# Twenty small unread products ahead of the second unit's mask

## The chip, the cores and the metric

The kernel runs on one core of a Trainium2 chip. The metric is the device time of one execution in microseconds (us): the kernel before takes 485.94 us, the median of three runs (485.89 to 486.22).

## The reference

Three layers follow one another. A windowed attention (4 batches, 8 heads, 576 positions, 64 wide; half of the heads look at the last 32 positions, half at every fourth of the last 128) gives 2304 tokens of 512. A gated layer makes `sigmoid(x @ w_gate) * (x @ w_val)` of 1536 and multiplies that with `w_out`. A soft mixture of 8 experts with 4 slots each follows:

```
scores = scale * (q @ k.T), masked;  x = softmax(scores) @ v
h = sigmoid(x @ w_gate) * (x @ w_val);  y = h @ w_out
logits = y @ phi;  d = softmax over tokens;  c = softmax over slots
out = c @ experts(d.T @ y)      # relu(. @ w1[e]) @ w2[e]
```

## The kernel before, in words

The tokens are worked through in five blocks (four of 512 tokens, a last one of 256). The attention of a block is four *units* of two heads. A unit is loaded as `qk` and `v` (L259 to L280). `scores` (L140) takes two banks of `ps_a` (four banks in all), lays the mask into each with a product against an identity in bfloat16 (L148), and adds 32 small float32 products, 32 x 64 each (L162). In the trace each of these is two passes, and each pass is a weight load and a product, so that the scores of a unit are 128 instructions for TensorE. `softmax` (L172) runs on VectorE and ScalarE, `turn_unit` (L191) transposes the weights through a bank (L195), and `weighted` (L198) makes 32 small products with `v` (L222), again 128 instructions. `finish_unit` (L227) splits the result into a high and a low part (L250, L251).

The gated layer is `l1` (L462): for a column tile `f` and for gate and value, twelve products of 128 x 512 (L474). Its weights arrive packed, are converted (`convert`, L371, on ScalarE, VectorE and GpSimd), stored, and loaded again (L365, L369, L866); all transfers are issued by SyncE in one queue. Between the two halves of a column tile `l1` calls a function that issues one step of the attention of the next blocks, so that from about 36 to 205 us TensorE alternates between a dozen large products and the two bursts of 128 small ones (scores of one unit, `weighted` of an earlier one). In the same stretch `slot_weights` (L404) adds transposes (L412), and small products (L418, L427). Blocks 2 and 3 are done as a pair with sums of halves (L606, L596), then the last block, and the experts with their weights (`load_e`, L816) end the program.

At the start there is nothing to interleave. `keep_warm` (L108) and L113 issue products of zeros until the first loads land. Then the four units of block 0 come one after the other, TensorE waiting for each unit's `qk`. A scheduler orders the instructions of each engine here; each engine then executes its own list in that order.

In what follows a *step* is one instruction of TensorE, a weight load or a product. The list of all steps lies in memory and is fetched by a DMA queue of its own (`q8 instruction` in the profile).

Of the kernel before, what the change touches and what calls it, by code (L numbers as in the profile page):

```python
# [31 lines left out]
C0 = 21  # L32
C1 = 19
WP = 1
ND = 4
M_ID, M_COLS = 768, 896
C_ID, C_I4, C_PHI, C_COLS = 0, 128, 256, 384
# [8 lines left out]
def k_window(n, hp, t, i):  # L46
    if n < 4:
        return 32 * (4 * t + i) if hp < 2 else 160 * i + 32 * t
    return 160 * t + 32 * i if hp < 2 else 64 * (4 * t + i)
# [7 lines left out]
def tile_kernel(  # L57
# [10 lines left out]
    nc = tc.nc  # L68
# [14 lines left out]
    def b8(tag, shape, dt, name):  # L83
        return big.tile(shape, dt, tag=tag, name=name, bufs=BUFS[tag])
# [6 lines left out]
    i4 = ones32[:, 0:32]  # L91
    phi = cst[:, C_PHI - C_ID : C_COLS - C_ID].rearrange("p (k s) -> p k s", k=ND)
    acc = cpool.tile([P, 3, 512], F32, name="acc")
# [14 lines left out]
    def keep_warm(count):  # L108
        for _ in range(count):
            nc.tensor.matmul(idle, lhsT=zero[:, 0:P], rhs=zero[:, 512:1024], start=True, stop=True)  # L110

    keep_warm(WARM)
    for i in range(SMALL):  # L113
        g = slice(32 * (i % 4), 32 * (i % 4) + 32)
# [18 lines left out]
    units = {}  # L133
# [3 lines left out]
    def at(ins):  # L137
        return tc.keep_in_program_order(ins) if grouped[0] else ins

    def scores(u, ts):  # L140
        n, hp = u["id"]
        q, k = u["qk"][:, 0:512], u["qk"][:, 512:1536]
        if "s_ps" not in u:
            u["bank"] = [ps_a.tile([P, 512], F32, tag="a", name=f"s_ps{r}") for r in range(2)]
            u["s_ps"] = [x[:, 0:256].rearrange("p (t c) -> p t c", t=4) for x in u["bank"]]
            for r in range(2):
                at(
                    nc.tensor.matmul(  # L148
                        u["s_ps"][r].rearrange("p t c -> p (t c)"),
                        lhsT=msk[:, M_ID:M_COLS],  # L150
                        rhs=mask[:, 2 if n == 4 else (1 if hp >= 2 else 0)],
                        start=True,
                        stop=False,
                        skip_group_check=True,
                    )
                )
        for t in ts:
            for i in range(4):
                for r in range(2):
                    o = k_window(n, hp, t, i)  # L160
                    at(
                        nc.tensor.matmul(  # L162
                            u["s_ps"][r][32 * i : 32 * i + 32, t, :],
                            lhsT=q[64 * r : 64 * r + 64, 128 * t + 32 * i : 128 * t + 32 * i + 32],
                            rhs=k[64 * r : 64 * r + 64, o : o + 64],
                            start=False,
                            stop=True,
                            skip_group_check=True,
                        )
                    )  # L170
# [56 lines left out]
    def finish_unit(u):  # L227
# [3 lines left out]
        def part(x, y):  # L231
            return x[:, hp].rearrange("p (t y x) -> p t y x", t=2, y=2)[:, :, y]

        if n in (2, 3):
            if n not in xf:
                xf[n] = b8("xa", [P, ND, 512], F32, "xf")
            nc.scalar.copy(part(xf[n], 0), xp[0])
            nc.vector.tensor_copy(part(xf[n], 1), xp[1])
            return
        if n not in x_hi:  # L240
            if n == 4:
                x4 = b8("x4", [P, 2, ND, 256], F32R, "x4")
                x_hi[n], x_lo[n] = x4[:, 0], x4[:, 1]
            else:
                tag = "xb" if n % 2 else "xa"
                x_hi[n] = b8(tag, [P, ND, 512], F32R, "x_hi")
                x_lo[n] = b8(tag, [P, ND, 512], F32R, "x_lo")
        for y in range(2):
# [10 lines left out]
    def attn_steps(pbs, norm, head=None):  # L259
# [34 lines left out]
        def s_step(z, ts=range(4)):  # L294
            if z == 0 and 0 in ts:
                if head:
                    load_qk(0)
                    ld(nc.sync.dma_start(msk, masks.bitcast(BF16)))
                    load_qk(1)
                    ld(nc.sync.dma_start(cst, consts))  # L300
                    load_v(0)
                    load_qk(2)
                    load_v(1)
                    head()
                    load_qk(3)
                    load_v(2)
                    load_v(3)
                else:
                    first(load_qk)
                    first(load_v)  # L310
            scores(us[z], ts)
            if 3 not in ts:
                return
            if 2 <= z and not head:
                weighted(us[z - 2], range(2), us[z])
            softmax(us[z], norm)
            load(z + 2, load_qk)
            if z == 0:
                load(2, load_v)
# [4 lines left out]
        def p_step(z, ts=range(2)):  # L324
            if head or z + 2 >= len(us):
                weighted(us[z], ts)
            if head:
                keep_warm(WP)
            if 1 in ts:
# [74 lines left out]
    def slot_weights(f, wo_f, lag):  # L404

        wt = pm.rearrange("p a b -> p (a b)").rearrange("p (k c x) -> p k c x", k=ND, c=2)
        at_ = {}
# [573 lines left out]
    for f in range(NF):  # L981
        for j in range(2):
            ins = T.matmul(
                lt_ps[32 * j : 32 * j + 32],
                lhsT=wp[:, f],
                rhs=g_sb[4, f][:, P * j : P * j + P],
                start=(f == 0),
                stop=(f == NF - 1),
# [96 lines left out]
    for f in range(NF):  # L1085
# [3 lines left out]
                lhsT=acc[:, f // 4, P * (f % 4) : P * (f % 4) + P],  # L1089
                rhs=i4w,  # L1090
                start=True,
                stop=True,
# [29 lines left out]
    for e in range(8):  # L1122
        for h in range(2):
            for kc in range(ND):
                ins = T.matmul(  # L1125
                    h_ps[h][32 * kc : 32 * kc + 32],
                    lhsT=st[:, kc, 32 * e : 32 * e + 32],
                    rhs=ew[0, e, h][:, kc],
                    start=(e == 0),
                    stop=(e == 7),  # L1130
# [227 lines left out]
```

## Time and profile before

| | |
|---|---|
| median of three runs | 485.94 us |
| profiled execution, its own time | 487.55 us |
| its span, first to last instruction | 485.8 us |
| TensorE products busy (PE) | 465.4 us, 96% |
| TensorE weight loads (PEld) | 358.1 us, 74% |
| VectorE, ScalarE, GpSimd | 64%, 44%, 32% |
| mean granted TensorE clock | 0.987 |

Busy products overlap, so 96% does not mean that TensorE runs at its peak. The granted clock is 1.00 or 0.50 of full speed in a stretch. "<-issue" behind an idle time means that the engine waited for nothing that the profile shows as an instruction or a transfer of data.

### The profile page before, as it was taken

What the parts mean: (1) busy time and instruction counts of PE and PEld (TensorE: products, weight loads), DVE (VectorE), ACT (ScalarE), POOL (GpSimd) and SP (SyncE); (2) the same over time, 40 slices, a digit from 0 to 9 for tenths busy, and PEclk for the clock granted to TensorE, in tenths of its full rate; (3) what the DMA queues carried; (4) which work ended last, traced back from release to release, by engine and by line L of the source; (5) the groups of instructions that cost most, each with busy time, mean ns of one, the idle gap of its engine ahead of it and who ended that gap; (6) DMA issues with size and microseconds to landing.
All of it is one profiled execution on the core that took longest, in us unless ns stands there. A gap on an engine that the chain in (4) does not pass through costs nothing.

```text
span 485.8 us, 12812 instructions
## 1 busy us (share of the span) xinstructions
PE 465.4 (96%) x5480; PEld 358.1 (74%) x5480; DVE 310.2 (64%) x629; ACT 213.6 (44%) x413; POOL 155.5 (32%) x132
## 2 busy tenths in 40 slices
PE   6789999999999999999999999999999999999993
PEld 3567888778777878787778888888888889842552
DVE  3869888758688666466876656656547765532623
ACT  2455555444455553454355554554535334300222
POOL 0244455325554564612033333324211124210100
PEclk9889999999999999999999999999999999999997
DMA  8978969994989792222220220201499886689976
GB/s 314 418 279 315 354 240 325 323 326 154 373 301 357 243 337 99 88 88 71 105 77 12 86 66 22 88 12 74 144 376 424 356 316 236 236 320 352 427 260 241
DMA packets 23721, 112.14 MB, mean 231 GB/s; under 512 B 2288, under 2 KB 7152, under 8 KB 14576
## 3 DMA queue, kind: packets, MB, share of 16 engines
q1 hardware_dynamic: 23664, 111.32, 62.0%
q8 instruction: 43, 0.70, 0.6%
q14 instruction: 14, 0.11, 0.1%
HBM read 97.16 MB, written 14.16 MB: 229 GB/s over the span
## 4 chain that ended last, share of the span: by engine, by line
PE 73%; DVE 4%; issue 2%; ACT 2%; POOL 2%; DMA 1%; DVEq 0%; ACTq 0%; POOLq 0%
PE l1ps L474 21%; PE pa L596 13%; PE pe L596 6%; PE tp L729 4%; PE so_ps L1187 3%; PE pd L596 3%; PE h_ps L1125 3%; PE sp L754 2%; PE lt_ps L700 2%; PE s_ps L222 2%; PE s_ps L162 2%; POOL fw L386 1%; PE wt_ps L412 1%; PE tr L195 1%; PE op L1225 1%
## 5 line engine op out<-in xcount | busy, mean ns | idle before, releaser
L474 PE MATMUL l1ps<-x_hi,whl 128*128 128x512 f32 x384 | 130.0, 403 | 2.4 <-ACT x_hi L250 2.0
L474 PEld LDWEIGHTS l1ps<-x_hi,whl 128*128 128x128 f32 x384 | 72.2, 189 | 18.5 <-ACT x_hi L250 2.7
L474 PE MATMUL l1ps<-x_lo,whl 128*128 128x512 f32 x192 | 76.0, 396 | 0.0
L386 POOL TENSOR_TENSOR fw<-fw 128x512 int32<-128x512 int32 x36 | 49.0, 1368 | 63.5 <-DVE fw L385 27.5
L474 PEld LDWEIGHTS l1ps<-x_lo,whl 128*128 128x128 f32 x192 | 36.4, 190 | 6.7 <-DVE x_lo L251 0.2
L460 DVE SCALAR_TENSOR_TENSOR g<-g,l1ps 128x512 f32<-128x512 f32 (+1 forms) x36 | 21.4, 593 | 25.3 <-PE l1ps L474 25.1
L474 PE MATMUL l1ps<-x,whl 128*128 128x256 f32 x288 | 37.0, 285 | 0.0
L474 PEld LDWEIGHTS l1ps<-x,whl 128*128 128x128 f32 x288 | 35.4, 192 | 0.4 <-ACT whl L437 0.2
L484 ACT ACTIVATE g<-l1ps 128x512 f32<-128x512 f32 (+1 forms) x36 | 18.9, 526 | 33.9 <-PE l1ps L474 33.7
L438 POOL TENSOR_TENSOR whl<-w,whl 128x512 fp32r<-128x512 f32 x12 | 15.9, 1329 | 51.2 <-ACT whl L437 39.7
L383 ACT ACTIVATE fw<-st 128x512 f32<-128x512 f32 x36 | 22.9, 676 | 12.2 <-DMA st<-wd 12.2
L729 PEld LDWEIGHTS tp<-cst,g 128*128 128x128 f32 x192 | 21.3, 140 | 5.4 <-issue 4.1
L729 PE MATMUL tp<-cst,g 128*128 128x128 f32 x192 | 25.0, 275 | 0.0
L384 DVE TENSOR_SCALAR fw<-fw 128x512 uint32<-128x512 uint32 x36 | 23.4, 659 | 2.4 <-ACT fw L383 1.7
L438 POOL TENSOR_TENSOR whl<-wst,whl 128x512 fp32r<-128x512 f32 x12 | 16.3, 1359 | 26.7 <-ACT whl L437 21.7
L734 ACT COPY gt<-tp 128x512 f32<-128x512 f32 x24 | 14.1, 586 | 24.1 <-PE tp L729 21.4
L659 DVE TENSOR_TENSOR tm<-pe,tm 128x512 f32<-128x512 f32 x12 | 8.3, 692 | 24.6 <-PE pe L596 24.6
L385 DVE TENSOR_SCALAR fw<-st 128x512 int32<-128x512 uint32 x36 | 18.1, 534 | 7.5 <-DMA st<-wd 7.2
L438 DVE TENSOR_TENSOR whl<-fw,whl 128x512 fp32r<-128x512 f32 x24 | 20.6, 873 | 3.5 <-ACT whl L437 2.9
L176 DVE TENSOR_REDUCE mx<-s_ps 128x4 f32<-128x256 f32 x40 | 15.3, 414 | 10.1 <-PE s_ps L162 8.2
L437 ACT CAST whl<-fw 128x512 fp32r<-128x512 f32 x24 | 14.6, 620 | 15.0 <-POOL fw L386 10.5
L189 POOL TENSOR_TENSOR sm<-sm,su 128x512 f32<-128x512 f32 x12 | 14.6, 1218 | 18.6 <-DVE su L188 16.3
(481 smaller groups left out, 961.7 us busy)
## 6 DMA issues: line engine op xcount, KB each, us to landing
ew<-w SPq DMA_DIRECT2D x32, 1024.0 KB, 7.5
st<-wd SPq DMA_DIRECT2D x18, 1024.0 KB, 9.3
wst<-wg SPq DMA_DIRECT2D x12, 1024.0 KB, 6.5
v<-qkv SPq DMA_DIRECT2D x20, 512.0 KB, 6.0
wg<-fw SPq DMA_DIRECT2D x12, 512.0 KB, 7.7
w<-wg SPq DMA_DIRECT2D x6, 1024.0 KB, 6.7
qk<-qkv SPq DMA_DIRECT2D x10, 576.0 KB, 5.8
qk<-qkv SPq DMA_DIRECT2D x8, 528.0 KB, 5.0
```

Source lines behind the costliest of these rows:

```text
L176: nc.vector.tensor_reduce(mx[:, 4 * r : 4 * r + 4], u["s_ps"][r], AX.X, ALU.max)
L189: norm.tensor_tensor(s, s, su.unsqueeze(2).to_broadcast([P, 8, 64]), ALU.mult)
L383: nc.scalar.activation(top, st[:, c, 1].bitcast(F32), AF.Prelu, scale=2.0**-112, alpha=2.0**32)
L384: nc.vector.tensor_scalar(top.bitcast(U32), top.bitcast(U32), 3, None, ALU.logical_shift_left)
L385: nc.vector.tensor_scalar(low.bitcast(I32), st[:, c, 0], 2.0**-29, None, ALU.mult)
L386: nc.gpsimd.tensor_tensor(low.bitcast(I32), top.bitcast(I32), low.bitcast(I32), ALU.add)
L438: (nc.gpsimd if pool[h] else nc.vector).tensor_tensor(whl[:, 1, h], src[:, h], whl[:, 0, h].bitcast(F32), ALU.subtract)
L460: return nc.vector.scalar_tensor_tensor(g, g, 1.0, val, ALU.add, ALU.mult)
L474: nc.tensor.matmul(pt[:, 0:nt], lhsT=whl[:, w_, a, dc, :], rhs=x_[n][:, dc, :], start=first, stop=(dc == HP_ORDER[-1] and w_ == 1),)
L484: nc.scalar.activation(g, pt[:, 0:nt], AF.Tanh, scale=0.5)
L596: nc.tensor.matmul(pt, lhsT=w[:, w_, P * c : P * c + P], rhs=x_[:, c], start=first and c == 0 and w_ == 0 and x_ is hi, stop=c == 1 and w_ ...
L729: nc.tensor.transpose(tp[:, c], g_sb[self.n, 4 * q + c][:, P * j : P * j + P], ident)
```

## The change

Ahead of the mask of the second unit (block 0, position 1 of its order) twenty products of 32 x 8 are issued into columns 256 to 263 of the unit's two banks, which nothing reads. They multiply slices of the first unit's `qk`, which is in place by then. Each is float32, so two passes of a weight load and a product: 80 steps in all. The dictionary `units` only keeps the first unit at hand.

```diff
+PAD = 20
...
+    def pad_stream(banks, qk):
+        for i in range(PAD):
+            r, g = i % 2, i // 2 % 4
+            at(
+                nc.tensor.matmul(
+                    banks[r][32 * g : 32 * g + 32, 256:264],
+                    lhsT=qk[64 * r : 64 * r + 64, 32 * g : 32 * g + 32],
+                    rhs=qk[64 * r : 64 * r + 64, 512:520],
+                    start=True,
+                    stop=True,
+                    skip_group_check=True,
+                )
+            )
...
             u["s_ps"] = [x[:, 0:256].rearrange("p (t c) -> p t c", t=4) for x in u["bank"]]
+            units[n, u["z"]] = u
+            if (n, u["z"]) == (0, 1):
+                pad_stream(u["bank"], units[0, 0]["qk"])
```

On TensorE, at the end of the first unit's scores (banks `s_ps_191` and `s_ps_192`), the list before goes on with the mask of the second unit (banks 238 and 239):

```order
L162 MATMUL s_ps_191<-qk 32x64
L162 MATMUL s_ps_192<-qk 32x64
L148 LDWEIGHTS msk
L148 MATMUL s_ps_238<-msk 128x256
L148 LDWEIGHTS msk
L148 MATMUL s_ps_239<-msk 128x256
L162 MATMUL s_ps_238<-qk 32x64
```

The list of the changed kernel has the twenty products there (the lines of `scores` are numbered 18 higher):

```order
L180 MATMUL s_ps_191<-qk 32x64
L180 MATMUL s_ps_192<-qk 32x64
L145 MATMUL s_ps_238<-qk 32x8
L145 MATMUL s_ps_239<-qk 32x8
...
L166 LDWEIGHTS msk
L166 MATMUL s_ps_238<-msk 128x256
L166 LDWEIGHTS msk
L166 MATMUL s_ps_239<-msk 128x256
L180 MATMUL s_ps_238<-qk 32x64
```

Everything behind keeps its order on TensorE and stands 80 steps later in the list.

On VectorE, in the softmax of the first three units (`mx` is the maximum of a bank of scores, `su` a unit's sum), the list before has both sums, of units 0 and 1, ahead of the third unit's first maximum (bank 333):

```order
L178 TENSOR_TENSOR sm_172<-s_ps_239,mx 128x256 [waits DVE_49]
L186 TENSOR_REDUCE su<-sm_172 128x8 [waits Activation_49] x2
L187 TENSOR_SCALAR su<-su 128x8 [waits DVE_49]
L176 TENSOR_REDUCE mx<-s_ps_333 128x4 [waits PE_49]
L188 RECIPROCAL su<-su 128x8 [waits DVE_49]
```

In the changed kernel's list (the third unit's bank is 353 there) that maximum stands between the two sums:

```order
L196 TENSOR_TENSOR sm_172<-s_ps_239,mx 128x256 [waits DVE_49]
L204 TENSOR_REDUCE su<-sm_172 128x8 [waits Activation_49]
L194 TENSOR_REDUCE mx<-s_ps_353 128x4 [waits PE_49]
L205 TENSOR_SCALAR su<-su 128x8 [waits DVE_49]
L204 TENSOR_REDUCE su<-sm_172 128x8 [waits Activation_49]
L206 RECIPROCAL su<-su 128x8 [waits DVE_49]
```

The second unit's sum has moved behind a wait for the third unit's scores. ScalarE, GpSimd and SyncE keep their lists.

## Rows read from the trace of the kernel before

**Rows 1.** The page: busy time of TensorE, the instruction queue (packets, MB, share).

```profile
PE 465.4 (96%) x5480; PEld 358.1 (74%) x5480; DVE 310.2 (64%) x629; ACT 213.6 (44%) x413; POOL 155.5 (32%) x132
q8 instruction: 43, 0.70, 0.6%
```

**Rows 2.** Timeline of TensorE's products: start, us, operation, count [idle before].

```profile
11.82 0.90 PE L162 MATMUL s_ps<-qk 64*32 64x64 f32 x55 [0.65 <-issue]
23.93 0.42 PE L222 MATMUL xp<-pt_ring,v 64*64 64x32 f32 x13 [1.14 <-issue]
127.38 0.36 PE L222 MATMUL s_ps<-pt_ring,v 64*64 64x32 f32 x9 [0.68 <-issue]
155.84 0.30 PE L222 MATMUL s_ps<-pt_ring,v 64*64 64x32 f32 x2 [0.77 <-issue]
```

**Rows 3.** Stretches cut there: us; PE, PEld, DVE, ACT, POOL (count); PEclk; DMA; GB/s.

```profile
0.00:11.50 11.50, 7.63 (x223) 3.77 (x224) 4.65 (x12) 2.54 (x3) 0.20 (x4) 1.00 0.86 306
11.50:23.30 11.80, 9.46 (x255) 6.26 (x254) 9.58 (x27) 5.24 (x10) 2.67 (x2) 0.86 1.02 421
23.30:127.10 103.80, 100.56 (x1529) 80.38 (x1529) 80.20 (x162) 52.22 (x99) 46.31 (x35) 0.98 0.83 296
127.10:155.50 28.40, 27.69 (x509) 22.41 (x509) 24.46 (x48) 16.35 (x31) 14.30 (x12) 1.00 0.92 336
```

**Rows 4.** DMA view, 9.4 to 10.4 us: instruction queue's packets, MB, share.

```profile
q8 instruction: 1, 0.02, 6.1%
```

**Rows 5.** DMA view, 153.4 to 154.4 us.

```profile
q8 instruction: 1, 0.02, 5.9%
```

**Rows 6.** DMA view, 140 to 146.8 us (it has no row of the instruction queue).

```profile
DMA packets 402, 2.36 MB, mean 348 GB/s; under 512 B 39, under 2 KB 39, under 8 KB 188
```

**Rows 7.** DMA view, 146.9 to 148 us.

```profile
q8 instruction: 1, 0.02, 5.5%
```

**Rows 8.** Stretches around the two times of lower granted clock.

```profile
8.90:12.30 3.40, 1.37 (x62) 0.82 (x63) 2.61 (x7) 0.78 (x2) 0.00 (x0) 1.00 1.03 420
12.40:15.70 3.30, 3.30 (x28) 1.44 (x14) 2.98 (x10) 0.67 (x1) 0.00 (x0) 0.50 1.01 415
22.60:25.90 3.30, 1.85 (x30) 1.26 (x23) 2.40 (x7) 2.14 (x5) 0.00 (x0) 1.00 1.03 410
26.00:29.40 3.40, 3.40 (x59) 2.55 (x61) 3.34 (x7) 1.39 (x3) 2.15 (x2) 0.50 0.91 308
```

**Rows 9.** Timeline of TensorE's products in block 0's units.

```profile
6.75 0.39 PE L148 MATMUL s_ps<-msk 128*128 128x256 bf16 x2
7.86 0.86 PE L162 MATMUL s_ps<-qk 64*32 64x64 f32 x64 [0.71 <-DMA qk<-qkv]
8.65 0.61 PE L110 MATMUL idle<-pm 128*128 128x512 bf16 x2
10.85 0.32 PE L162 MATMUL s_ps<-qk 64*32 64x64 f32 x9 [1.38 <-DMA qk<-qkv]
15.61 0.67 PE L195 MATMUL tr<-cst,sm 128*128 128x128 f32 x4
```

**Rows 10.** Timeline of VectorE in the softmax of those units.

```profile
8.74 0.76 DVE L176 TENSOR_REDUCE mx<-s_ps 128x4 f32<-128x256 f32 x2 [0.35 <-PE s_ps L162]
13.53 0.69 DVE L189 TENSOR_TENSOR sm<-sm,su 128x512 f32<-128x512 f32 x1
```

**Rows 11.** Stretches of the middle: a pair of bursts, what follows it, and a later one.

```profile
143.10:145.55 2.45, 2.45 (x138) 1.88 (x136) 2.34 (x4) 0.51 (x1) 1.36 (x1) 1.00 0.99 403
145.55:152.82 7.27, 7.27 (x44) 6.05 (x40) 6.42 (x14) 5.66 (x11) 2.48 (x2) 1.00 1.00 415
172.50:174.00 1.50, 1.50 (x32) 1.42 (x26) 1.50 (x4) 0.07 (x1) 1.50 (x2) 1.00 0.75 212
```

**Rows 12.** Timeline of TensorE's products around 171 us.

```profile
170.88 0.86 PE L162 MATMUL s_ps<-qk 64*32 64x64 f32 x64
172.73 0.63 PE L427 MATMUL wp_ps<-cst,acc 128*128 128x32 f32 x4
```

## The prediction

> **What bounds the kernel now.** I read the page first, then the waits of TensorE, then its timeline and stretches cut where it stood still. TensorE's products are busy for 465.4 of 485.8 us [rows 1], and in the middle, where two bursts of 128 small steps alternate with large products, without a gap [rows 11]. So what TensorE loses there is lost at the end. In four places it stands in the middle of a burst and waits for nothing that the profile knows: "<-issue" of 0.65, 1.14, 0.68 and 0.77 us [rows 2].
>
> The reader is to see what these places have in common, by counting. Stretches cut inside the pauses hold 447, 509, 3058 and 1018 steps (PE plus PEld) [rows 3]. With 3, 14 and 6 further entries of the list, which the view doesn't count (I take them for the separate waits in front of products that wait for two engines), the last three are 512, 3072 and 1024: 2, 12 and 4 times 256. The instruction queue moves 0.70 MB in 43 packets, 16.3 KB each, against 10,960 steps, 255 per packet [rows 1]. So TensorE's list comes in blocks of 256 entries, and each pause is the wait for the next block. I number the boundaries from the first pause: 0, 2, 14 and 18 paused the engine.
>
> When is a block late? One is fetched between 9.4 and 10.4 us [rows 4], 6.1% of 16 engines over 1 us, so 0.98 us long, and TensorE goes on at 11.82, 1.4 us after it; one between 153.4 and 154.4 [rows 5], and TensorE goes on at 155.84 [rows 2], 1.4 us after it again. So a block can be executed 2.4 us after its fetch begins. The fetch begins when TensorE has passed the boundary before, or later: boundary 17 lies at the mask at 152.8 (counting 256 entries back from 155.84), and the fetch at 153.4 followed by 0.6 us; boundary 16 lies 256 entries further back, past the 84 steps of 145.55 to 152.82 and 172 of the 274 before them, so some 100 steps into that pair of bursts, 143.6 [rows 11], and the fetch that followed came at 146.9 [rows 6, 7], 3.3 us later, at a DMA share of 0.99. A block that is executed in less than 3.0 to 5.7 us pauses the engine; a pair of bursts, 256 steps, takes 2 us.
>
> [...]
>
> **The change part by part.** The twenty products: 64 passes of L162 take 0.86 us [rows 9], so 40 take 0.54. They stand behind the first unit's scores, ahead of the mask at 6.75 [rows 9], and the 0.71 us wait for the second unit's load covers them: 0, and 0.54 if the cover were gone. They wait for nothing new. All that follows keeps its order, but each boundary now falls 80 entries earlier in the work. I go through all 42 and compare, in the timeline, when TensorE gets there with the earliest time of the block.
>
> *Removed.* Boundaries 14 and 18 move 80 steps up, still in the same burst, and the boundary before moves too, so that the block between them begins among the large products: block 18 then runs from L412 at 145.6 [rows 11] into the burst that ends at 156, over 8 us, and block 14 likewise. The pauses of 0.68 and 0.77 go: -1.45. Nothing else is late there, TensorE being gapless.
>
> *Block 0, boundary 0.* It stood 19 steps into the third unit's scores and now stands 75 steps into the second's, reached at 7.86 + 75/128 of 0.86 = 8.4. The boundary before lies ahead of the new products, so the fetch stays at 9.4 and TensorE goes on at 11.8, as before. That is 3.4 us of standing, where before 1.38 went for a load and 0.65 for the block; at 11.8 it owes 80 steps more: 53 of the second unit, fillers (0.61), mask, 19 of the third, some 1.5 us at the lower clock that follows. VectorE, whose list is executed in order, gets the second unit's scores at 12.2 in place of 8.74 [rows 10], then has two maxima (0.76), two subtractions (0.75), the first sum (as wide as the multiply, 0.69), and by its new order a wait for the third unit's scores, near 14.5, ahead of the second sum and two further maxima (0.69, 0.76). The multiply at 13.53 comes near 16.7, its transposes near 17.4 in place of 15.61 [rows 9], and the conversions queue behind. Lag near 20 us: 2 to 3. Boundary 2, which cost 1.14, is then met late and close to its fetch, and gives back about 1. I take +1.5 for all up to 36 us; bounds -1.1 (lag absorbed, the pause gone) and +4 (all kept, and a longer stretch at the lower clock).
>
> *Boundary 17.* It stood at the mask at 152.8, and between 145.55 and 152.82 lie 84 steps, counting those under way [rows 11]. So it now stands at the transposes L412 at about 145.6, just behind a pair of bursts, and the boundary before at about 143.2, where the pair begins: 274 steps in 143.10 to 145.55 [rows 11]. The whole block is executed in 2.45 us. [...] Begin 145.7 to 147.0, block ready 148.1 to 149.4, pause 2.5 to 3.8. A lower bound is a fetch that begins after 0.6: ready at 146.2, pause 0.6. I take 3.2, by the nearest row: +3.2.
>
> *The clock behind it.* [...] Half speed for 3.4 us of gapless work costs 1.7; bounds 0 and 2.5 (two stretches touched). +1.7.
>
> *Boundary 21.* It now falls at L427, about 173.1, and the one before at the start of a pair of bursts, 170.9 [rows 12]. A fetch 0.6 to 3.3 us after gives a block at 173.9 to 176.6 and a pause of 0.8 to 3.5; the DMA share falls to 0.75 at 172.5 [rows 11], so I let it begin at 172.3: ready 174.7, +1.6. Lower clock behind it, which the 0.7 us pauses did not bring and rows 8 make possible, 0.5 (0 to 1.7).
>
> The other boundaries meet their blocks in time; 3, 4, 9 and 33 have the least to spare.
>
> Sum: -1.45 + 1.5 + 3.2 + 1.7 + 1.6 + 0.5 = +7.05. The profiled execution took 487.55 us, 1.75 around its span, and 1.6 more than the median of the runs; 487.55 becomes 494.6, and the median 485.94 becomes 493.0. By the terms' bounds the likeliest case's own range is 489.5 to 496.5.
>
> **Rivals.** First, the same mechanism with a worse start: VectorE's lag of 3 us isn't given back at boundary 2, both pauses leave two stretches at the lower clock. Head +4, boundary 17 3.8 + 2.5, boundary 21 2.2 + 1.7, less 1.45: +12.7, 498.7; with half of these extras 496.5 to 498.5. For it: VectorE is busy for 2.61 of 3.40 us early on [rows 8]; against: TensorE waits there for loads anyway.
>
> Second, faster: the fetch for boundary 17. It decides at 145.6 - 2.4 = 143.2 us: if the sequencer reads far enough ahead, in the large products, that the fetch begins by then, block 17 costs nothing, boundary 21 likewise (its fetch by 170.7), and if the head comes out level the two pauses (1.45) and the 1.14 at boundary 2 are gone: 483.4, and 481.7 if the lower clock at 26 us goes with its pause. For it: the fetch at 153.4 took 0.6 us. Against: the one asked for in this very burst took 3.3.
>
> Third, no change: the pauses come from the traffic of their moments, not from a count, and stay: 0 + 0, 485.9. Against: the counts come out at 2, 12 and 4 times 256. [...]
>
> **How the numbers follow.** The forecast 0.62; the worse start 0.15; faster 0.11; no change 0.06; and 0.06 for a small loss (boundary 17 at its lower bound, no lower clock), 486.9 to 489.5. Faster by over 0.2% (0.97 us, about what a measurement of this kernel tells from no change) is then 0.11, within it 0.06, slower 0.83. Predicted 493.0. The range leaves out the faster case and the upper half of the worse start: 485.7 to 498.0.
>
> **What would show it.** Right: "<-issue" inside the second unit's scores from about 8.4 to 11.8; none near 126 and 155 (times shifted); a pause of some 3 us in front of L412 behind a pair of bursts near 146, with a granted clock of 0.50 after it; one of 1 to 2 us at L427 near 175; counts between pauses at multiples of 256 again. Wrong: block 17 met without a pause, or pauses at the old places in the work.

## The result, and the profile after

The changed kernel takes 489.93 us, the median of six runs (488.62 to 492.25), beside 486.08 of the kernel before in six runs on the same chip (485.47 to 487.83). The ratio is 1.0068, with an interval of 1.0041 to 1.0095: slower, by 3.3 us by the ratio and 3.85 by the medians. Forecast were 7.05 more, 493.0, in 485.7 to 498.0: the sign and the range held, the size is half.

The profiled execution took 492.25 us (span 490.5, mean granted clock 0.980), the highest of the six; that of before took 487.55 (0.987). So the two traces differ by 4.70 us, more than the medians do.

The page after, TensorE and the instruction queue, to set beside [rows 1]:

```profile
PE 467.8 (95%) x5520; PEld 358.9 (73%) x5520; DVE 310.9 (63%) x629; ACT 213.5 (44%) x413; POOL 155.2 (32%) x132
q8 instruction: 43, 0.70, 0.5%
```

There are 80 steps more, and nothing else. The pauses are found in the timeline of TensorE's products after (columns as in [rows 2]):

```profile
7.05 0.57 PE L145 MATMUL s_ps<-qk 64*32 64x8 f32 x37
7.55 0.39 PE L166 MATMUL s_ps<-msk 128*128 128x256 bf16 x2
7.87 0.62 PE L180 MATMUL s_ps<-qk 64*32 64x64 f32 x37
12.37 0.67 PE L180 MATMUL s_ps<-qk 64*32 64x64 f32 x27 [3.87 <-issue]
22.50 0.49 PE L492 MATMUL l1ps<-x_hi,whl 128*128 128x512 f32 x1 [1.41 <-ACT x_hi L268]
128.19 1.13 PE L240 MATMUL s_ps<-pt_ring,v 64*64 64x32 f32 x64
147.14 0.33 PE L430 MATMUL wt_ps<-cst,fw 128*128 128x128 f32 x1
148.93 0.55 PE L430 MATMUL wt_ps<-cst,fw 128*128 128x128 f32 x3 [1.46 <-issue]
157.25 1.14 PE L240 MATMUL s_ps<-pt_ring,v 64*64 64x32 f32 x64
174.96 0.84 PE L445 MATMUL wp_ps<-cst,acc 128*128 128x32 f32 x4
```

The second unit's scores are cut after 37 of 64 products, for 3.87 us. The bursts that were cut near 127 and 155 run as 64 products in one piece (128.19, 157.25). A new pause stands behind the first product of L430 (L412 before), and none at L445 (L427 before).

The stretches after, cut at the first pause and at the one near 148, to set beside [rows 3]:

```profile
0.00:10.00 10.00, 7.04 (x223) 3.73 (x224) 2.00 (x5) 1.91 (x2) 0.20 (x4) 1.00 0.78 273
10.00:22.00 12.00, 8.05 (x235) 4.88 (x234) 8.45 (x21) 3.71 (x7) 1.77 (x2) 0.72 1.02 420
22.00:148.20 126.20, 121.52 (x1931) 96.94 (x1931) 100.73 (x204) 64.35 (x123) 57.49 (x44) 0.99 0.84 301
```

The first holds 447 steps, as before. From there to the pause at 148.2 there are 469 + 3862 = 4331, and 17 times 256 are 4352. The 21 that are left are semaphore waits in TensorE's list, which the stretches don't count: the trace after has 2 and 19 of them here (that of before 3, 14 and 6, as the prediction took). The two pauses are boundaries 0 and 17.

Stretches after around boundary 17, the pair of bursts first, to set beside [rows 11]:

```profile
144.60:146.70 2.10, 2.10 (x134) 1.85 (x136) 2.10 (x5) 1.90 (x4) 1.29 (x2) 1.00 1.02 414
147.50:148.90 1.40, 0.00 (x0) 0.00 (x0) 1.40 (x4) 0.00 (x0) 0.04 (x1) 1.00 1.04 391
149.00:152.40 3.40, 3.40 (x18) 2.83 (x19) 2.41 (x8) 1.96 (x5) 0.00 (x0) 1.00 1.01 417
```

TensorE does nothing in the pause, and the granted clock stays 1.00 behind it. The DMA view after, 145.7 to 146.7 us (first line, no row of the instruction queue) and 146.7 to 147.7:

```profile
DMA packets 87, 0.43 MB, mean 434 GB/s; under 512 B 12, under 2 KB 12, under 8 KB 56
...
q8 instruction: 1, 0.02, 5.8%
```

The fetch begins at 146.75, 2.0 us behind the scores of its pair (144.72), and TensorE goes on 2.2 us later.

How much later the same instruction starts in the trace after than in the trace before, by its time in the latter (worked out from both timelines):

| at (before) | later by | what came since |
|---|---|---|
| 36 us | +3.03 | the start |
| 118 | +2.50 | a wait of 0.39 at L474, 104.4 in before, is not there after |
| 135 | +1.59 | boundary 14 no longer pauses: -0.91 |
| 153 | +3.31 | boundary 17: +1.73 |
| 161 | +2.23 | boundary 18 no longer pauses: -1.08 |
| 182 | +2.44 | boundary 21: +0.2, no pause |
| 408 | +2.37 | nothing |
| 470 | +4.71 | 411 to 437 us: a pause of 0.40 (+0.65), a lower clock (+1.69) |

The last line has little to do with the change. A stretch after:

```profile
433.60:436.80 3.20, 3.20 (x20) 0.87 (x16) 0.00 (x0) 0.00 (x0) 0.00 (x0) 0.50 0.29 49
```

Here the granted clock was 0.50. A later run (before without four loads, below) has TensorE's list of before word for word, and the same there:

```profile
431.70:434.90 3.20, 3.20 (x20) 0.65 (x12) 0.00 (x0) 0.00 (x0) 0.00 (x0) 0.50 0.35 123
```

### The profile page after: what moved, and what is told of

It reads as the page before. It is cut to its first block, busy times and chain, and to the rows that moved or that the text cites. A ratio compares the mean times of both kernels' runs of the same rounds, so it can differ in the third digit from the quotient of the medians.

```text
span 490.5 us, 12892 instructions
## 1 busy us (share of the span) xinstructions
PE 467.8 (95%) x5520; PEld 358.9 (73%) x5520; DVE 310.9 (63%) x629; ACT 213.5 (44%) x413; POOL 155.2 (32%) x132
## 4 chain that ended last, share of the span: by engine, by line
PE 87%; DVE 4%; DMA 2%; ACT 2%; issue 2%; POOL 1%; ACTq 0%; DVEq 0%; POOLq 0%; SPq 0%
PE l1ps L492 30%; PE pa L614 13%; PE pe L614 6%; PE tp L747 4%; PE s_ps L180 3%; PE so_ps L1205 3%; PE pd L614 3%; PE s_ps L240 3%; PE h_ps L1143 3%; DMA w<-wg 2%; PE sp L772 2%; PE lt_ps L718 2%; PE tr L213 2%; PE wt_ps L430 1%; PE s_ps L166 1%
## 5 line engine op out<-in xcount | busy, mean ns | idle before, releaser
L180 PE MATMUL s_ps<-qk 64*32 64x64 f32 x1280 | 18.1, 233 | 3.9 <-issue 3.9
```

The costliest lines, as they stand in the source:

```text
L180: nc.tensor.matmul(u["s_ps"][r][32 * i : 32 * i + 32, t, :], lhsT=q[64 * r : 64 * r + 64, 128 * t + 32 * i : 128 * t + 32 * i + 32], rhs=k ...
```

## The experiments

The theory: the number of steps ahead of a place decides which pauses there are, whatever the steps are. Rivals: the added products themselves, or VectorE's changed order, cost the time at the start. Behind that stands a second question: when is the next block asked for?

**Twelve products in place of twenty** (48 steps).

```diff
-PAD = 20
+PAD = 12
```

> Twelve unread products in place of twenty: 48 steps. Every engine but TensorE keeps the list of the kernel before (VectorE's swap is not there). Theory (place of the block boundaries): boundary 0 still lies in the second unit's scores (107 steps in), so TensorE stands there from about 8.6 to 11.9-12.3 us and is 2.3 to 2.8 us late at 36 us; the pauses of the kernel before in the bursts near 126 and 155 are gone (-1.9); the blocks near 60, 85 and 146 us, close to late by 0.4 to 0.7, are covered by that lag. Total +0.5 to +1.0, 486.6 to 487. Rival (VectorE's swap makes the lag at the start): no lag at 36 us, total 484 to 484.5.

Measured: 488.29 us, ratio 1.0053 (1.0032 to 1.0074). VectorE's list is that of before here. TensorE stands for 3.81 us in the second unit's scores, and its lag (how much later than before it runs) is 1.58 us at 36; the pauses near 126 and 155 are gone, one of 0.44 stands behind boundary 17. So the long standstill needs no change on VectorE.

**Five products** (20 steps).

```diff
-PAD = 20
+PAD = 5
```

> Five unread products: 20 steps, all other lists as before. Theory: boundary 0 falls at the end of the second mask-and-filler stretch, just ahead of the third unit's scores, where TensorE waits for a load until 10.85 anyway: no pause in the second unit's scores, TensorE goes on at 11.8, lag at 36 us 0 to 0.4. The pause near 126 us goes (-0.9), the one near 155 shrinks to about 0.4, a new one of up to 1.2 near 58 us. Total -0.5 to +0.6, 485.6 to 486.7. Rival (any product ahead of the mask costs at the start): lag of 2 us or more, 488.

Measured: 485.12 us, 0.9988 (0.9968 to 1.0008). The pause near 126 is gone, that near 155 is 0.62, and the new one expected near 58 did not come; the start's lag is -0.2. TensorE is 2.07 us ahead up to 428 us, and the profiled run loses 1.7 of it to a lower clock at 428.4 to 431.8.

**Eighty steps further on**: the twenty products stand ahead of the first unit of block 1, with that unit's own `qk`.

```diff
-            units[n, u["z"]] = u
-            if (n, u["z"]) == (0, 1):
-                pad_stream(u["bank"], units[0, 0]["qk"])
+            if u["id"] == (1, 0):
+                pad_stream(u["bank"], u["qk"])
```

> The same twenty products, 80 steps, but ahead of the scores of block 1's first unit (near 35.5 us), multiplying that unit's own qk: the start is as before, the boundaries behind it fall as in the changed kernel. Theory (a fetch begins when the transfers queued ahead of it have drained, so the pause depends on how late TensorE is against the transfers): lag at 40 us 0.5 (the products, uncovered); pauses near 126 and 155 us gone (-1.9); the pause at L412 near 146 us is 2.7 to 3.5, longer than the changed kernel's 1.46, as TensorE comes 2 us earlier; 0 to 1.7 for a lower clock behind it; a pause of 0.5 to 1.5 at L427 near 173. Total +2 to +4, 488 to 490. Rival (a block is ready a fixed 4 us after it is asked for): the pause stays 1.5, none at 173, total 0 to +0.2, 486.2.

Measured: 490.29 us, 1.0079 (1.0052 to 1.0106). The start is that of before. The pauses near 126 and 155 are gone, and these stand in the timeline (L429, L444 are L412, L427 of before):

```profile
148.59 0.90 PE L429 MATMUL wt_ps<-cst,fw 128*128 128x128 f32 x3 [1.82 <-issue]
177.11 0.19 PE L444 MATMUL wp_ps<-cst,acc 128*128 128x32 f32 x1 [0.61 <-issue]
```

Behind the first the granted clock is 0.50:

```profile
146.80:148.50 1.70, 0.00 (x0) 0.00 (x0) 1.70 (x4) 0.00 (x0) 0.42 (x1) 0.92 1.00 390
148.60:151.50 2.90, 2.90 (x9) 2.42 (x10) 1.58 (x5) 1.90 (x4) 0.00 (x0) 0.50 1.04 422
```

At 153 us the lag is 4.34 (0.88 at 144): 1.82 of pause and some 1.6 of clock. These are the two terms which the prediction added for this place (3.2 + 1.7); the clock's came as forecast, the pause is little over half, and below the 2.7 to 3.5 expected of this run. And the loss in the middle comes without the start.

**Eighty steps at the very front**: no products in the banks, but forty more fillers of zeros.

```diff
-SMALL = 70
+SMALL = 110
...
+        w = 32 if i < 70 else 16
-        nc.tensor.matmul(idle[g, 0:32], lhsT=zero[:, 0:32], rhs=zero[:, 512:544], start=True, stop=True)
+        nc.tensor.matmul(idle[g, 0:w], lhsT=zero[:, 0:32], rhs=zero[:, 512 : 512 + w], start=True, stop=True)
```

> No unread products; forty more products of zeros (32 x 16) in the row that keeps TensorE busy at the start, 80 steps ahead of the first unit. TensorE's list is else the same, VectorE's and ScalarE's differ in a few swaps of conversions, VectorE's sums as in the kernel before. Theory (only the count matters): boundary 0 lies 75 steps into the second unit's scores again, TensorE stands there until 11.1 to 12.4 us, pause near 147 at L412 and none near 126 and 155; total +2.5 to +4, 488.6 to 490. Rival (the products or their place ahead of the mask): as before but for 0.3 us at the start, 486.3.

Measured: 491.74 us, 1.0105 (1.0085 to 1.0125). The timeline, with the same breaks as after (x27, x3):

```profile
11.55 0.67 PE L163 MATMUL s_ps<-qk 64*32 64x64 f32 x27 [3.09 <-issue]
147.81 0.55 PE L413 MATMUL wt_ps<-cst,fw 128*128 128x128 f32 x3 [1.39 <-issue]
175.63 0.19 PE L428 MATMUL wp_ps<-cst,acc 128*128 128x32 f32 x1 [1.30 <-issue]
```

This settles the first question: other instructions, in another place, give the same pauses at the same steps, without VectorE's swap at the second unit's sum (its list differs from that of before in a few conversions and maxima behind 16 us). The count decides where a pause can stand. Whether one comes there is not decided by it alone: in the four other profiles whose boundaries lie where they lie in before (they follow below), boundary 14 pauses for over 0.3 us in two (1.23 and 1.28), boundary 18 in two (0.71 and 0.52).

**Six products** (24 steps), a number chosen to let most blocks be in time.

```diff
-PAD = 20
+PAD = 6
```

> Six unread products: 24 steps, all other lists as in the kernel before. Theory: boundary 0 falls into the two fillers behind the second unit's scores (TensorE then waits for the third unit's load anyway), so no lag at 36 us (-0.3 to +0.3); boundary 14 has moved into the start of its burst and costs nothing; boundary 18 moves 4 steps further up than with five products (pause there 0.62) and costs 0 to 0.5. Total -1.5 to -2, 484.3 to 484.8. Rival (the gain of five products is chance): the same as before, 486.3.

Measured: 485.44 us, 0.998 (0.9959 to 1.0002). No such pause of 0.3 us or more is left between 20 and 180 us; the one at 155 has become

```profile
153.35 0.43 PE L240 MATMUL s_ps<-pt_ring,v 64*64 64x32 f32 x14 [0.19 <-issue]
```

The profile is 1.8 to 2.4 us ahead of before from 140 us to the end. In the medians 0.9 is left, and the interval touches 1: by its profile the best of all, but not shown to be faster.

**Sixteen products** (64 steps), with VectorE's order as in the changed kernel.

```diff
-PAD = 20
+PAD = 16
```

> Sixteen unread products: 64 steps, VectorE's swap as in the changed kernel. At the start the third unit's maximum ahead of the second unit's sum is the only other difference to twelve products (lag at 36 us 1.58 there). Theory (the lag comes from where boundary 0 lies, 91 steps into the second unit's scores): lag 1.6 to 2.0 and 0.1 more for 16 steps. Rival (VectorE's swap matters): lag 2.5 to 3.1, as in the changed kernel (3.03). Boundary 17 stands among the large products behind L412 near 146: a pause of 1.0 to 1.5 if its fetch comes 2.0 us after TensorE has passed the boundary before (as with twenty products), 2.5 to 3.0 if 3.5 us after (as with none, five or twelve).

Measured: 488.15 us, 1.0027 (0.9997 to 1.0058). Standstill 3.79, lag 1.97 at 36 us, beside 1.58 with twelve products and VectorE's old order. On VectorE, from the second unit's first maximum to the multiply that waits for the sums (L207) it is 3.98 us here (12.29 to 16.27), and 3.60 with twelve products (12.20 to 15.80): the swap is worth 0.4 us. The pause at boundary 17 is 0.54, where 1.0 to 1.5 or 2.5 to 3.0 was expected.

**Sixty-four products further on** (256 steps, one whole block), at the place of the third experiment.

```diff
-PAD = 20
+PAD = 64
...
+            if u["id"] == (1, 0):
+                pad_stream(u["bank"], u["qk"])
```

> Sixty-four unread products, 256 steps, ahead of block 1's first unit (near 35.5 us), one whole block. Theory (only the count modulo 256 matters): every later boundary falls where it falls in the kernel before, with the next block: pauses of 0.6 to 0.8 return after 55 of 64 passes of L222 near 127 and after 62 of 64 near 156, none near 147 at L412; lag 0.9 to 2.5 (64 products at 27 ns a pass are 1.7 us, less what TensorE waited there, and possibly one pause inside the products), total +1 to +2.5. Rival (the products themselves, by what they do, remove or make pauses): pauses as with eighty steps late, one at L412, none near 127 and 156.

Measured: 489.82 us, 1.0064 (1.0036 to 1.0092). The pause of boundary 14 is back at the very step it had before, 9 products from the end of the burst, and L412 has none:

```profile
129.67 0.36 PE L239 MATMUL s_ps<-pt_ring,v 64*64 64x32 f32 x9 [1.23 <-issue]
```

The one near 155 did not come back, so a boundary at the same step doesn't always pause. At 36 us it is 2.5 late, with the products and three stretches of lower clock, 18.4 to 28.7 us, ahead of that.

**The unit's load asked for later**, no products: each `qk` a step later in the program, to move it away from boundary 16.

```diff
-            load(z + 2, load_qk)
+            if z == 0:
+                load(2, load_qk)
...
                 load(z + 3, load_v)
+            load(z + 3, load_qk)
```

> No unread products; the load of qk for the unit after next is asked for in the step that transposes the unit before, some 5 us later than behind the scores, so that it isn't issued in the middle of a pair of bursts. TensorE's list is that of the kernel before, SyncE's is another. Theory (a fetch waits for the transfers issued ahead of it, and the qk issued 0.9 us after a pair of bursts begins is among them unless the fetch is asked for at the pair's very start): the fetch for boundary 17, 3.4 us after its request in the kernel before, comes 2.0 to 2.5 us after, at 145.5 to 146; pauses at boundaries 14 and 18 change by their own traffic. Rival (the delay depends on the place in the burst alone): 3.3 to 3.6 again. Total -1 to +1.

Measured: 487.77 us, 1.0029 (1.0003 to 1.0054). Inconclusive: the load waits for its buffer (in before such loads, L273, waited 14 times for the scores of L162, 78.9 us in all), and was issued at 144.43, 0.9 us behind the beginning of its pair as ever; only `v` had moved, to 139.27. The fetch came 3.9 us behind the pair.

**One load left out, before and after.** One line of `load_qk` reuses the tile, one skips the transfer.

```diff
-            us[z]["qk"] = b8(tags[z], [P, 2048], F32, "qk")
+            us[z]["qk"] = us[11]["qk"] if z == 12 else b8(tags[z], [P, 2048], F32, "qk")
...
-            ld(nc.sync.dma_start(us[z]["qk"][:, 0:w], ...
+            z == 12 or ld(nc.sync.dma_start(us[z]["qk"][:, 0:w], ...
```

> The kernel before, in which the 13th of the sixteen later units computes its scores from the qk of the unit ahead of it, so that its own load (576 KB, issued at 144.03 us in the trace of before) is left out; every engine's list but SyncE's stays as it was. Disputed: why the block of boundary 17 is fetched 3.6 to 4.0 us after the pair of bursts near 143 us begins in some kernels and 1.8 to 2.3 us in others. Theory one, the fetch waits behind the unit's loads when it is asked for behind them: 0.58 MB less at about 400 GB/s are 1.4 us, so the fetch comes 2.0 to 2.8 us after the pair begins. Theory two, TensorE's sequencer asks later and the loads have nothing to do with it: 3.6 to 4.0 us as in the kernel before. Time: within 1 us of the kernel before by either, since no boundary pauses there; the pause of 0.77 us near 155 stays by theory two and becomes nothing by theory one only if boundary 18's own fetch moves too, which neither says.

> The changed kernel with the same load left out (issued there at 145.61 us, 0.9 us after the pair begins, and 1.1 us ahead of the fetch of boundary 17). Theory one, the fetch was asked for ahead of the load and did not wait for it: it comes 1.8 to 2.3 us after the pair begins, the pause at L430 stays at 1.2 to 1.8 us. If the load did delay it too: up to 1.4 us earlier, a pause of 0 to 0.5 us. Theory two: 1.8 to 2.3 us and 1.2 to 1.8 us too. Time: 0 to 1.5 us below the changed kernel's.

Measured, one run each, beside 486.82 us for the kernel before: 487.26 and 493.44. In the first the next unit's load took the place at 143.70 us, and the fetch came at 147.3, 4.5 behind the pair's scores (142.81); against theory one, but with a load still in the way. In the second it came 1.3 us behind them, the pause is 0.94, between the ranges expected, and one of 0.68 stands at L445.

**Four loads left out, before and after.** The same two lines with `z >= 12`, and unit 11 loaded 1536 columns wide.

```diff
-            w = 512 + k_cols(n, hp)
+            w = 1536 if z == 11 else 512 + k_cols(n, hp)
```

> The kernel before, with the last four of the sixteen later units all computing their scores from the qk of the unit ahead of them (loaded 1536 columns wide), so that no qk load is issued behind about 135 us: in the run with one load less the next unit's load took its place at 143.70 us, 0.9 us behind the beginning of the pair of bursts. TensorE's and VectorE's lists are those of the kernel before. Theory one, the fetch of boundary 17 waits behind the load that the pair's scores release: with none it begins at most 2.8 us after the pair's scores begin (142.5 to 143.5 us, so by 146.3). Theory two, the sequencer asks so late, whatever the loads are: 3.6 to 4.5 us after, as in the kernel before (3.8) and in the run with one load less (4.5).

> The changed kernel with the same four loads left out. Theory one, the fetch was asked for ahead of the load: as in the changed kernel (2.0 us after the pair's scores begin) and with one load less (1.3 us), so 1.0 to 2.3 us; the pause in front of the second L430 product 0.5 to 1.8 us. Theory two the same. A pause of nothing there would say that the qk load, not the count of steps, makes block 17 late.

Measured, one run each: 490.26 and 494.34 us. In the first, the pair's scores, and the instruction queue from 148 to 149 us; 144.7 to 148.2 has no row of it:

```profile
144.70 0.86 PE L162 MATMUL s_ps<-qk 64*32 64x64 f32 x64
```

```profile
q8 instruction: 1, 0.02, 5.5%
```

SyncE issues nothing from 142.9 to 150 us, and still the fetch begins at 148.4, 3.7 behind the scores. Theory one falls: it isn't the load released by the pair that delays it. But transfers issued earlier (`v`, the weights) are still under way, and up to the fetch they fill the engines, as the DMA view from 144.7 to 148.2 us shows (packets, MB, share of 16 engines):

```profile
q1 hardware_dynamic: 265, 1.38, 98.3%
```

In the second the fetch came 2.5 us behind the pair, a little outside the range expected, the pause was 2.13 (0.5 to 1.8 expected), and the clock fell behind it:

```profile
148.80:150.80 2.00, 0.00 (x0) 0.00 (x0) 2.00 (x5) 0.00 (x0) 0.39 (x1) 1.00 1.00 410
151.50:154.80 3.30, 3.30 (x9) 2.60 (x8) 1.59 (x4) 1.88 (x4) 0.00 (x0) 0.50 1.02 427
```

The totals expected were mostly missed, and to the long side: 488.29 us for 486.6 to 487 with twelve products, 490.29 for 488 to 490 with eighty steps further on, 491.74 for 488.6 to 490 with eighty at the front, 485.44 for 484.3 to 484.8 with six products, 3.5 more than before for 1 to 2.5 with 256 steps, and with one load left out after 493.44, where at most the changed kernel's 489.93 was expected. What follows rests on the traces.

The fetch of boundary 17 in all profiles (18 with 256 steps), from the start of its pair's scores. Boundary 16 lies about 100 steps into that pair in before (by the prediction's count), and as many fewer as steps were added:

| steps added | boundary 16, steps into the pair | fetch behind the start, us |
|---|---|---|
| 0 (four lists), 256 | 100 | 3.9, 3.9, 4.5, 3.7; 3.6 |
| 20, 24, 48 | 80, 76, 52 | 4.0, 3.6, 3.8 |
| 64 | 36 | 2.3 |
| 80 (five lists) | 20 | 2.0, 2.2, 1.8, 1.3, 2.5 |

Sixteen steps are passed in 0.1 us here (128 in 0.79), yet between 52 and 36 the fetch moves by 1.4 us. The loads left out move it within a group, by up to 0.8 us, never across. The two groups are those of this boundary: for boundary 21 the boundary before lies 91 steps into a pair in the list of before, and the fetch comes 2.1 us behind the pair's start there, 2.5 and 1.6 with one and four loads left out.

What makes the step is open, and the transfers under way as a whole are not ruled out: in all these profiles they fill the engines ahead of this fetch (a share of 0.99 from the start of the pair's scores to the fetch in before, 1.07 after). Where they moved nothing, a fetch came 0.8 us behind the boundary before it. Boundary 12 of the kernel before is passed at 116.8 us (by counting 254.8 steps per block) and its next fetch begins at 117.62; the DMA view of 116.8 to 117.6 us:

```profile
DMA packets 0, 0.00 MB, mean 0 GB/s; under 512 B 0, under 2 KB 0, under 8 KB 0
```

Counted so between 36 and 205 us in all 14 profiles, the fetch began at most 1.3 us behind the boundary before (once 1.7) where the engines were under 15% busy from 1 us ahead of that boundary up to the fetch (68 cases), and up to 6.4 us behind it where they were over 90% busy (143 cases). No experiment emptied the engines at boundary 17, so that the long waits come from the traffic is likely, but not shown.

## Why the prediction was right in sign and wrong in size

*Right.* The list comes in blocks of 256 entries (4352 from boundary 0 to 17, 17 times 256), and the change moves each boundary 80 steps up in the work: the same steps were cut with quite other instructions added. The pauses of boundaries 14 and 18 went, worth 0.91 and 1.08 for the 1.45 forecast. The standstill began at 8.50 for 8.4 forecast, and boundary 17 pauses at L412. The rival of no change is out. In the whole trace after, with its 43 blocks, TensorE's products show "<-issue" at two boundaries alone, 0 with 3.87 us and 17 with 1.46.

*The step that failed* is in the term of boundary 17: the fetch of before, asked for in the same burst, came at 146.9 [rows 7], and that after was to begin 145.7 to 147.0 with the engine there at 145.6, a pause of 3.2. That range was the author's estimate, which no run shows; the trace after, less its lag of 1.6 us, has the fetch at 145.2. A fetch time seen with boundary 16 at one place of the pair was carried to another place, 80 steps up: at this boundary the fetch comes 3.6 to 4.5 us behind the pair's start with 0 to 48 steps added, and 1.3 to 2.5 with 80, at full engines in both. The unit's own loads don't make the difference (3.7 without them in the list of before); what does is open. So the pause is 1.46 after and 0.94 to 2.13 in the five lists with 80 steps: the lower half of the bounds (0.6 to 3.8), from which the value by the nearest row was the wrong choice.

*The clock behind it*: 0 after for 1.7 forecast. The term took one stretch of the lower clock, as in [rows 8], behind the pause. The runs show one behind some pauses and not behind others: the clock stayed at 1.00 behind 1.46, 1.39 and 0.94 us, and was 0.50 behind 1.82 and 2.13. Boundary 17 together: 1.73 for 4.9.

*Boundary 21*: 0.2 for 1.6 + 0.5. TensorE reaches it at 175 as forecast, but the fetch begins at 173.2, 0.1 us behind its pair's scores (173.11), in place of the 1.4 taken. It is a near thing: with 80 steps three other lists pause there, for 0.61, 0.68 and 1.30.

*The start* was too small: 3.03 after for 1.5, still within its bounds of -1.1 to 4. The block's fetch began at 10.2, not 9.4, and the lower clock held from 10.2 to 17.1 us, twice as long as the first such stretch of before [rows 8]. The lag was 3.5 us at 20 us and 2.2 at 30, behind boundary 2, as the prediction had it; but it was 3.0 again at 36. The two other runs with this start are at 4.0 and 3.4, those with 48 and 64 steps at 1.6 and 2.0, the one with 80 steps at the front at 1.7; VectorE's swap, which the prediction had for the culprit, explains 0.4 of that. The granted clock was at its lower level for 10.2, 13.6 and 13.6 us ahead of 36 us in the three with the larger lag, for 6.8 in those with 48 and 64 steps, but for 10.2 too in the one with 1.7: what sets the rest is open.

*Not forecast*: 0.5 us given back between 36 and 118 us, and 2.3 lost behind 408, of which 1.7 is a lower clock that a list of before shows as well.

By the terms, to 408 us: 3.03 - 0.53 - 0.91 + 1.73 - 1.08 + 0.2 - 0.07 = 2.37 in the profiled pair, for 7.05. The errors had both signs: 3.2 too much at boundary 17, 1.9 at 21, 0.5 at the removed pauses; 1.5 too little at the start. The medians' 3.85 lies above the 2.37; with one profile each the rest is not apportioned.

## What to carry to other kernels

Where TensorE runs long bursts of short instructions, count its steps between pauses that wait for "nothing": if they come at multiples of one number (256 here), an added instruction anywhere ahead moves all that follow (80 steps in three places each brought a pause at the transposes L412, of 1.46, 1.82 and 1.39 us), and a change of 20 to 80 steps has to be judged by where the boundaries fall, not by what its instructions cost (0.5 us here). A few dead steps can be a cheap correction (with 24 none of 0.3 us or more was left between 20 and 180 us), but the next edit upstream moves the boundaries again. A delay seen once at one place should not be carried to a place that differs in position, even by 0.4 us: take its bounds.

## What the runs showed of the hardware

- The fetch for boundary 17 comes in two groups, 1.3 to 2.5 and 3.6 to 4.5 us behind the start of a pair of bursts, by where the boundary before falls in it; the groups don't carry over to boundary 21 (2.1 in before, 0.1 after).
- With the engines near idle a fetch began at most 1.3 us behind the boundary before, once 1.7 (0.8 at boundary 12 of before); between 36 and 205 us, waits of over 2 us stand only where they were at least half busy.
- A lower clock does not follow a pause by its length alone: 1.28 us near 126 brought it in the run with four loads left out, 1.40 near 92 (the third experiment) and 1.46 near 148 did not. The first of these:

```profile
126.20:127.30 1.10, 0.00 (x0) 0.00 (x0) 0.00 (x0) 0.00 (x0) 0.00 (x0) 1.00 0.95 396
127.90:131.10 3.20, 3.20 (x8) 2.50 (x8) 3.06 (x6) 1.24 (x2) 1.62 (x2) 0.50 1.08 398
```

- The same list differs from run to run by up to 1.6%: the kernel before took 483.96 to 491.69 us in the 50 runs beside the experiments that were timed.
